# Sliding-window attention in four 64x64 tiles of the array, with the products with v beside the scores

## The chip, the cores and the metric

The kernel runs on one core of one Trainium2 chip. The metric is device time in microseconds of one execution, and less is better. A core has a matmul engine (TensorE, PE in the profile), a vector engine (VectorE, DVE), an engine for activations (ScalarE, ACT), a general one (GpSimd, POOL) and SyncE (SP), which here issues transfers. Matmuls write to PSUM, eight banks of 512 float32 columns in each of 128 partitions; everything else lives in SBUF.

## The reference

Attention with a sliding window of 128 and a linear distance penalty, then a gated feed-forward block. There are 8 batches of 8 heads, 576 positions and head dimension 64; the feed-forward width is 1536. Inputs and outputs are float32.

```python
scores = (q @ k.T) / sqrt(64) - slope[h] * abs(i - j)      # slope[h] = 2 ** -(h + 1)
scores = where((i - j >= 0) & (i - j < 128), scores, -1e9)
attn = softmax(scores)
x = (attn @ v) with heads side by side                     # 4608 tokens x 512
out = (gelu(x @ w_gate) * (x @ w_val)) @ w_out             # 4608 x 512
```

The window means that a key at position j meets only queries j to j + 127.

## The kernel before

Everything is in bfloat16 with float32 sums. The tokens go through the feed-forward block in nine groups of 512: a gate stage of 12 steps (`gate_val`, eight matmuls of 512 columns each) and an out stage (`out_part`, 16 units of three matmuls). The attention of the next batches is threaded between these. Scores are kept with keys on partitions and queries along the columns, so the exponentials serve as moving operand for the products with v without a transpose. Two heads lie over each other: `qT[64 * i : 64 * i + 64, c]` is head 2c + i.

Keys come in blocks of 128. A block meets 256 queries, and each head is one 64x128 tile, two of which run side by side:

```python
SCORES = (((0, 0, 256, 0), (1, 128, 256, 256)),          # key block, first query, queries, column
          ((2, 256, 256, 512), (3, 384, 192, 768), (4, 512, 64, 960)),
          ((2, 256, 256, 512), (3, 384, 128, 768), (3, 512, 64, 896), (4, 512, 64, 960)))

def scores(b, s, cs, then=None, later=None):
    for c in cs:
        ps = [bank(), bank()]
        for j, q0, n, col in SCORES[...]:
            for i in (0, 1):
                score(b, c, i, j, q0, n, ps[i][:, ...])
    ...                                     # per head pair: two exps of 512, one masking multiply
```

`exp` is an activation on ScalarE out of PSUM; `mask` multiplies by exp(-slope * distance), zero outside of the window, on VectorE. `add` adds on VectorE what two key blocks give to the same queries, so that the sums of the softmax need fewer matmuls:

```python
def sums(b, s):                             # column tiles of 128x32
    ...
    nc.vector.reciprocal(row(b)[:, lo:hi], ps[:, 0:hi - lo])

def gather(b, n=S):                         # reciprocals to DRAM
def spread_dma(b, n=S):                     # and back, broadcast over 64 partitions each

def products(b, s, cs):                     # 128x64 tiles, two side by side
    for c in cs:
        ps = bank()
        for n, (j, a, e, col) in enumerate(pieces):
            for i in (0, 1):
                h = 2 * c + i
                nc.tensor.matmul(out=ps[64 * i:64 * i + 64, a - lo:e - lo],
                                 lhsT=vb[b % 2][:, j, 64 * h:64 * h + 64],
                                 rhs=P[:, c, i, col:col + e - a], ...)
```

`values` multiplies the products by the reciprocals on VectorE and writes xT, the input of the gate stage. In batches 1 and 2 and in the first one the reciprocals are spread by small float32 matmuls (`spread4`, `sums4`) instead.

For batches from 2 on, q and k are loaded by GpSimd in five transfers each, converted on the way, and transposed by SyncE's transfer queue:

```python
def transposes_dma(b):
    for src, dst in ((ks, kT), (qs, qT)):
        nc.sync.dma_start_transpose(out=dst[b % 2]..., in_=src[b % 2]...)
```

The out stage of group g carries this (a number is that many out units; "s" are scores of batch, half and head pairs):

```python
todo = {
    0: [("s", 1, 0, (0, 1)), 4, ("s", 1, 0, (2, 3)), 2,
        ("s", 1, 1, (0, 1), None, masks), ("add", 1, 0), 2, ("sum4", 1, 0), ("masks",),
        ("s", 1, 1, (2, 3)), 4, ("spread4", 1, 0, acts), ("transposes", 2),
        ("sum4", 1, 1, False), ("pv", 1, 0), 2, ("spread4", 1, 1, acts), ("pv", 1, 1), 2],
    ...}
# groups 3 to 5, b = g + 2
    [("s", b, 0, (0, 1, 2)), 6, ("s", b, 0, (3,)), ("add", b, 0),
     ("s", b, 1, (0, 1)), ("add", b, 1, (0, 1)), 6, ("s", b, 1, (2, 3)), ("add", b, 1, (2, 3)), 4]
```

In those groups `sums` stands after gate step 1, `gather` after 3, `spread_dma` after 5, and the products with v after steps 8 and 10, two head pairs each.

Of the kernel before, what the change touches and what calls it, by code (L numbers as in the profile page):

```python
# [7 lines left out]
FP32 = mybir.dt.float32  # L8
# [10 lines left out]
SCORES = (((0, 0, 256, 0), (1, 128, 256, 256)),  # L19
          ((2, 256, 256, 512), (3, 384, 192, 768), (4, 512, 64, 960)),  # L20
          ((2, 256, 256, 512), (3, 384, 128, 768), (3, 512, 64, 896), (4, 512, 64, 960)))


PIECES = ((((0, 0, 256, 0), (1, 128, 384, 256), (2, 256, 384, 512)),
           ((2, 384, 512, 640), (3, 384, 576, 768), (4, 512, 576, 960))),
          (((0, 0, 256, 0), (1, 128, 256, 256)),
           ((2, 256, 512, 512), (1, 256, 384, 384), (3, 384, 576, 768), (4, 512, 576, 960))))
# [5 lines left out]
def kernel(  # L33
# [48 lines left out]

    slope1 = consts.tile([128, H], BF16, name="slope1")
    slopes = wo[:, 0:2, :].rearrange("p a (h x) -> p (a h) x", x=128)
    dist = wo[:, 2, 0:256]
    ones = consts.tile([128, 2, 32], BF16, name="ones")
    ones4 = consts.tile([128, 8 * 36], BF16, name="ones4")
    ones8 = consts.tile([128, 4 * 40], BF16, name="ones8")


    emask = consts.tile([128, H, 512], BF16, name="emask")
    sel0 = consts.tile([128, 8], FP32, name="sel0")
    sel = consts.tile([128, 8, 64], FP32, name="sel")
# [3 lines left out]
    qs, ks = ([consts.tile([128, 5, DM], BF16, name=f"{nm}s{i}") for i in range(2)]  # L97
# [8 lines left out]
    def load(t, src, b, js=range(5)):  # L106
        for j in js:
            n = rows(j)
            nc.gpsimd.dma_start(  # L109
                out=t[0:n, j, :].rearrange("p (h d) -> p h d", h=H),  # L110
                in_=src[b][:, 128 * j:128 * j + n, :].rearrange("h p d -> p h d"))

    def load_qk(b):
        load(qs[b % 2], q, b)
        load(ks[b % 2], k, b)

    def load_v(b, js=range(5)):
        load(vb[b % 2], v, b, js)
# [5 lines left out]
    def runs(what, b, n):  # L124
        first, parts, r = RUNS[b][n]
        t, lo, p = (qs, ks)[what][b], 1536 * n, 0
        if (b, n) == (0, 1):
            t, lo, p = vb[1], 0, 64 * what
        return t.rearrange("p j x -> p (j x)")[p:p + parts, lo:lo + 512 * r].rearrange(
            "p (h x) -> p h x", h=H)  # L130
# [40 lines left out]
    def transposes_dma(b):  # L171
        for src, dst in ((ks, kT), (qs, qT)):
            nc.sync.dma_start_transpose(
                out=dst[b % 2].rearrange("p c (j t) -> p (c j) t", t=128),
                in_=src[b % 2].rearrange("p j x -> p (j x)"))


    def columns(t, b, i, c, at, n):
        lo = 64 * i
        if b < 2:  # L180
            return t[b][lo:lo + 64, c, at:at + n]
        blocks = t[b % 2].rearrange("p c x -> p (c x)").rearrange(
            "p (j c t) -> p j c t", j=5, c=4)
        j = at // 128
        if n <= 128:
            return blocks[lo:lo + 64, j, c, at - 128 * j:at - 128 * j + n]
        return blocks[lo:lo + 64, j:j + n // 128, c, :]

    probs, both = {}, {}

    def prob(b):
        if b not in probs:
            probs[b] = p_pool.tile([128, 4, 2, 1024], BF16, name="P")
        return probs[b]

    def score(b, c, i, j, q0, n, out):
        rhs = columns(qT, b, i, c, q0, n)
        if rhs.ndim == 3:
            out = out.rearrange("p (n t) -> p n t", t=128)
        nc.tensor.matmul(out=out, lhsT=columns(kT, b, i, c, 128 * j, 128), rhs=rhs,  # L200
                         start=True, stop=True)
# [7 lines left out]
    def scores(b, s, cs, then=None, later=None):  # L209
        pss = []  # L210
        for c in cs:
            ps = [bank(), bank()]
            pss.append(ps)
            for j, q0, n, col in SCORES[s if b < 2 or s == 0 else 2]:
                for i in (0, 1):
                    score(b, c, i, j, q0, n, ps[i][:, col - 512 * s:col - 512 * s + n])
        if then:
            then()
        P = prob(b)
        for c, ps in zip(cs, pss):  # L220
            dst = P[:, c, :, 512 * s:512 * s + 512]
            for i in (0, 1):
                exp(dst[:, i, :], ps[i])
            if s == 0:
                args = (dst.rearrange("p i (n x) -> p i n x", n=2),
                        emask[:, 2 * c:2 * c + 2, 0:256].unsqueeze(2).to_broadcast(
                            (128, 2, 2, 256)))
            else:
                args = (dst, emask[:, 2 * c:2 * c + 2, :])
            if later is None:  # L230
                mask(*args)
            else:
                later.append(args)

    def bias(h, ps, n, start=True):
        d = dist.unsqueeze(1).to_broadcast((128, n, 256)) if n > 1 else dist[:, 0:128].unsqueeze(1)
        nc.tensor.matmul(out=ps.rearrange("p (n x) -> p n x", n=n),
                         lhsT=slopes[:, h, :], rhs=d, start=start, stop=False,  # L240
                         skip_group_check=True)

    def added(c, i, j, q0, n, out):
        nc.tensor.matmul(
            out=out, lhsT=columns(kT, 0, i, c, 128 * j, 128), rhs=columns(qT, 0, i, c, q0, n),
            start=False, stop=True, skip_group_check=True)


    def biases0(cs, idle=0):
        pss = []  # L250
        for c in cs:
# [3 lines left out]
            for i in (0, 1):  # L255
                bias(2 * c + i, ps[i], 2)
        return pss

    def scores0(cs, pss):
        for c, ps in zip(cs, pss):  # L260
            for j, q0, col in ((0, 0, 0), (1, 128, 256)):
                for i in (0, 1):
                    added(c, i, j, q0, 256, ps[i][:, col:col + 256])
# [5 lines left out]
    def scores0_rest(cs, later):  # L269
        pss = []  # L270
        for c in cs:
            ps = [bank(), bank()]
            pss.append(ps)
            for j, q0, n, col in ((2, 384, 128, 0), (3, 384, 192, 128), (4, 512, 64, 320)):
                for i in (0, 1):
                    score(0, c, i, j, q0, n, ps[i][:, col:col + n])
        P = prob(0)
        for c, ps in zip(cs, pss):
            for i in (0, 1):
                exp(P[:, c, i, 640:1024], ps[i][:, 0:384])  # L280
            later.append((P[:, c, :, 640:1024], emask[:, 2 * c:2 * c + 2, 128:512]))


    def biases0_2():
        pss = [bank(), bank()]
        for c in range(4):
            for i in (0, 1):
                bias(2 * c + i, pss[i][:, 128 * c:128 * c + 128], 1, c == 0)
        return pss

    def scores0_2(pss):
        for c in range(4):
            for i in (0, 1):
                added(c, i, 2, 256, 128, pss[i][:, 128 * c:128 * c + 128])
        for i in (0, 1):
            exp(prob(0)[:, :, i, 512:640], pss[i].rearrange("p (c n) -> p c n", c=4))
# [3 lines left out]
    def add(b, s, cs=range(4)):  # L300
        if b not in both:
            both[b] = s_pool.tile([128, 8, 448], BF16, name="S")
        lo, hi = 2 * cs[0], 2 * cs[-1] + 2
        P = prob(b).rearrange("p c i n -> p (c i) n")[:, lo:hi, :]
        T = both[b][:, lo:hi, :]

        def plus(out, in0, in1):
            nc.vector.tensor_tensor(out=out, in0=in0, in1=in1, op=ALU.add)  # L308

        if s == 0:  # L310
            plus(T[:, :, 0:128], P[:, :, 128:256], P[:, :, 256:384])
        else:
            by2 = P[:, :, 384:896].rearrange("p h (n y x) -> p h n y x", n=2, y=2)
            plus(T[:, :, 128:384].rearrange("p h (n x) -> p h n x", n=2),
                 by2[:, :, :, 0, :], by2[:, :, :, 1, :])
            plus(T[:, :, 384:448], P[:, :, 896:960], P[:, :, 960:1024])

# [13 lines left out]
    def shape(b, s):  # L331
        lo, hi = part(b, s)
        n = 4 if (b, s) == (0, 0) else 2
        return lo, (hi - lo) // n, n

    def sums4(b, s, added=True):
        first, w, count = shape(b, s)
        ps = bank()
        P, T = prob(b).rearrange("p c i n -> p (c i) n"), both.get(b)
        mms = []  # L340
        for h in range(H):
            for x in range(count):
                t = first + w * x
                g, lhsT = ((x, ones4[:, 32 * h:32 * h + 32]) if count == 4 else
                           (2 * x + h // 4, ones8[:, 32 * (h % 4):32 * (h % 4) + 32]))
                if added and t >= 128:
                    mms.append((g, lhsT, T[:, h, t - 128:t - 128 + w], 0, w, 0))
                elif added:
                    mms.append((g, lhsT, P[:, h, t:t + w], 0, w, 0))
                else:  # L350
                    for j, a, e, col in PIECES[min(b, 1)][s]:
                        lo, hi = max(a, t), min(e, t + w)
                        if lo < hi:
# [461 lines left out]
```

The softmax here doesn't subtract the row's maximum and nothing guards it: scores larger than these inputs give would overflow.

## Time and profile before

The median of three runs is 352.25 us (352.13 to 352.71). The profiled execution spans 350.6 us.

| stretch, us | what | length | PE busy | DVE busy | ACT busy |
|---|---|---|---|---|---|
| 0 to 18.66 | start, attention of batch 0 | 18.66 | 15.59 | 14.89 | 14.11 |
| 18.66 to 44.50 | gate stage of group 0 | 25.84 | 25.48 | 15.14 | 12.29 |
| 44.50 to 63.27 | out stage of group 0 | 18.77 | 18.65 | 13.60 | 13.84 |
| 63.27 to 104.97 | group 1 | 41.70 | 41.19 | 23.47 | 27.03 |
| 104.97 to 141.77 | group 2 | 36.80 | 36.80 | 25.80 | 22.42 |
| 178.19 to 214.61 | group 4 | 36.42 | 36.42 | 22.71 | 19.93 |
| 251.04 to 285.06 | group 6 | 34.02 | 34.02 | 15.61 | 10.80 |
| 285.06 to 316.14 | group 7, no attention | 31.08 | 31.08 | 8.30 | 9.51 |

The busy columns come from windows of the trace: time in which at least one instruction of that engine ran. A busy PE isn't a full PE, since the ends of its matmuls are modelled; what a stretch of it cost is read from the chain that ended last, where each piece runs until the next one starts. A group without attention lasts 31.08 us, so what a group lasts beyond that is its attention.

### The profile page before, as it was taken

The numbers are of one execution on the slowest core, as the hardware profiler recorded it, in microseconds if no ns is written. First come the engines' busy times: TensorE is split into PE (matmuls) and PEld (weight loads), VectorE is DVE, ScalarE is ACT, GpSimd is POOL, SyncE is SP. The second block draws the span as 40 slices with busy tenths as digits, with TensorE's granted clock in tenths as the row PEclk, the third lists the DMA queues.
The fourth block names the chain that finished last, engine by engine and source line by source line (L and its number), as shares of the span: only waits on it lengthen the run. The fifth ranks groups of instructions, "written<-read, shape, count | busy, mean of one in ns | idle before, by whom it ended". The sixth has DMA issues, their size and how long they took to land.

```text
span 350.6 us, 6847 instructions
## 1 busy us (share of the span) xinstructions
PE 343.2 (98%) x2756; PEld 171.4 (49%) x2756; DVE 193.6 (55%) x345; ACT 180.3 (51%) x332; POOL 105.7 (30%) x139
## 2 busy tenths in 40 slices
PE   8899999999999999999999999999999999999996
PEld 6665446444464445445444544454444544444443
DVE  6894467434878837856666655755684314303320
ACT  5963495535978374633863296328823123323322
POOL 9965480770850265003900292004000000000000
PEclk9999999999999999999999999999999999999999
DMA  9999999999999099984998399849206020021002
GB/s 180 173 197 190 202 154 165 187 152 160 144 152 182 3 168 182 197 164 54 155 226 148 68 145 196 179 93 97 92 6 133 30 90 3 1 82 39 0 30 90
DMA packets 148831, 43.00 MB, mean 123 GB/s; under 512 B 133784, under 2 KB 141720, under 8 KB 148800
## 3 DMA queue, kind: packets, MB, share of 16 engines
q0 software_dynamic: 108480, 18.49, 70.0%
q1 hardware_dynamic: 36976, 17.70, 21.3%
q10 hardware_dynamic: 3344, 6.38, 8.3%
q8 instruction: 21, 0.34, 0.4%
q14 instruction: 10, 0.08, 0.1%
HBM read 43.65 MB, written 9.53 MB: 152 GB/s over the span
## 4 chain that ended last, share of the span: by engine, by line
PE 91%; ACT 4%; DVE 3%; DMA 1%; issue 0%; ACTq 0%
PE ps L472 54%; PE ps L498 24%; PE ps L430 5%; PE ps L200 3%; ACT P L204 2%; PE ps L377 1%; PE ps L363 1%; DMA wo<-in_q_dram 1%; DVE P L207 1%; PE ps L399 1%; PE ps L514 1%; DVE S L308 1%; PE ps L152 0%; ACT qT L160 0%; ACT L204 0%; DVE xT L458 0%
## 5 line engine op out<-in xcount | busy, mean ns | idle before, releaser
L479 DVE TENSOR_TENSOR hT<-ps,gelu 128x512 bf16<-128x512 f32 (+3 forms) x112 | 73.8, 668 | 101.8 <-PE ps L472 94.8
L478 ACT ACTIVATE gelu<-ps 128x512 bf16<-128x512 f32 (+3 forms) x112 | 64.5, 582 | 114.8 <-PE ps L472 113.3
L472 PE MATMUL ps<-xT,wg 128*128 128x512 bf16 (+3 forms) x448 | 112.2, 372 | 0.5 <-DVE xT L444 0.2
L472 PE MATMUL ps<-xT,wv 128*128 128x512 bf16 (+3 forms) x448 | 111.6, 371 | 0.0
L498 PE MATMUL ps<-wo,hT 128*128 128x512 bf16 x420 | 95.6, 380 | 0.0
L204 ACT ACTIVATE P<-ps 128x512 bf16<-128x512 f32 (+1 forms) x130 | 65.9, 612 | 5.9 <-PE ps L200 4.9
L472 PEld LDWEIGHTS <-wv 128*128 128x128 bf16 x448 | 43.3, 98 | 50.3 <-issue 0.2
L472 PEld LDWEIGHTS <-wg 128*128 128x128 bf16 x448 | 42.0, 98 | 49.2 <-issue 1.8
L498 PEld LDWEIGHTS <-hT 128*128 128x128 bf16 x420 | 39.0, 98 | 46.5 <-issue 1.7
L207 DVE TENSOR_TENSOR P<-P,emask 128x1024 bf16<-128x1024 bf16 (+1 forms) x60 | 39.5, 679 | 24.1 <-ACT P L204 23.8
L503 ACT COPY osb<-ps 128x512 f32<-128x512 f32 x32 | 19.2, 599 | 35.4 <-PE ps L498 33.1
L109 POOL DMA_DIRECT2D vb<-in_v_dram x40 | 33.9, 883 | 3.9 <-DMA ks<-in_k_dram 1.9
L444 DVE TENSOR_TENSOR xT<-ps,rb 128x320 bf16<-128x320 f32 (+2 forms) x64 | 23.0, 423 | 11.4 <-DMA rb<-rd 6.8
L765 POOL COPY mark<-hT 1x2 bf16<-1x2 bf16 x4 | 0.7, 174 | 89.8 <-DVE hT L479 89.8
L109 POOL DMA_DIRECT2D qs<-in_q_dram x30 | 25.2, 857 | 7.4 <-DMA wo<-in_moe_w_out_dram 5.5
L109 POOL DMA_DIRECT2D ks<-in_k_dram x30 | 25.4, 891 | 6.1 <-DMA qs<-in_q_dram 6.0
L200 PE MATMUL ps<-qT,kT 64*128 64x256 bf16 (+3 forms) x352 | 18.6, 236 | 1.2 <-DVE xT L458 0.5
L404 DVE RECIPROCAL r<-ps 128x256 f32<-128x256 f32 (+1 forms) x10 | 18.8, 1921 | 0.0
L430 PE MATMUL ps<-P,vb 128*64 128x256 bf16 (+3 forms) x384 | 17.5, 239 | 0.0
L200 PEld LDWEIGHTS <-kT 64*128 64x128 bf16 x352 | 12.1, 94 | 11.1 <-issue 8.8
L430 PEld LDWEIGHTS <-vb 128*64 128x64 bf16 x384 | 14.7, 110 | 5.1 <-issue 4.6
L308 DVE TENSOR_TENSOR S<-P 128x1024 bf16<-128x1024 bf16 (+3 forms) x27 | 15.1, 590 | 0.5
(82 smaller groups left out, 138.3 us busy)
## 6 DMA issues: line engine op xcount, KB each, us to landing
out_dram<-osb SPq DMA_DIRECT2D x35, 256.0 KB, 3.5
rb<-rd ACTq DMA_DIRECT2D x10, 576.0 KB, 7.4
vb<-in_v_dram POOLq DMA_DIRECT2D x32, 128.0 KB, 6.3
qs<-in_q_dram POOLq DMA_DIRECT2D x24, 128.0 KB, 6.2
ks<-in_k_dram POOLq DMA_DIRECT2D x24, 128.0 KB, 6.3
wo<-in_moe_w_out_dram POOLq DMA_DIRECT2D x2, 768.0 KB, 14.7
wg<-in_moe_w_gate_dram POOLq DMA_DIRECT2D x5, 256.0 KB, 8.4
wv<-in_moe_w_val_dram POOLq DMA_DIRECT2D x5, 256.0 KB, 9.0
```

The source lines that it names most:

```text
L109: nc.gpsimd.dma_start(out=t[0:n, j, :].rearrange("p (h d) -> p h d", h=H), in_=src[b][:, 128 * j:128 * j + n, :].rearrange("h p d -> p h d"))
L200: nc.tensor.matmul(out=out, lhsT=columns(kT, b, i, c, 128 * j, 128), rhs=rhs, start=True, stop=True)
L204: nc.scalar.activation(out=dst, in_=src, func=AF.Exp, scale=0.125)
L207: nc.vector.tensor_tensor(out=dst, in0=dst, in1=m, op=ALU.mult)
L404: nc.vector.reciprocal(row(b)[:, lo:hi], ps[:, 0:hi - lo])
L430: nc.tensor.matmul(out=ps[64 * i:64 * i + 64, a - lo:e - lo], lhsT=vb[b % 2][:, j, 64 * h:64 * h + 64], rhs=P[:, c, i, col:col + e - a], s ...
L444: nc.vector.tensor_tensor(out=xT[:, c, at:at + e - a], in0=ps[:, a - lo:e - lo], in1=recip[b][:, c, a:e], op=ALU.mult)
L472: nc.tensor.matmul(out=ps, lhsT=w[:, c, 128 * f:128 * (f + 1)], rhs=xT[:, c, t0 + lo:t0 + hi], start=(c == 0), stop=(c == 3))
L478: nc.scalar.activation(out=gl[:, 0:n], in_=pg, func=AF.Gelu)
L479: nc.vector.tensor_tensor(out=hid[g][:, f, lo:hi], in0=pv, in1=gl[:, 0:n], op=ALU.mult)
L498: nc.tensor.matmul(out=acc[g], lhsT=hid[g][:, f, 128 * t:128 * (t + 1)], rhs=wo[:, f, :], start=(f == 0), stop=(f == NF - 1))
L503: (nc.vector.tensor_copy if t == 0 and g < 2 or t == 1 and g == 0 else nc.scalar.copy)(out=osb, in_=acc[g])
```

## The change

Keys are taken in nine blocks of 64 instead of five of 128. A block of 64 meets 192 queries, so less of what is computed falls outside of the window: 1664 columns of 64 keys for a head instead of 1024 of 128. A score matmul contracts over 64 and gives 64 keys, and so fills a quarter of the array: two heads by two key blocks run in four 64x64 tiles. The products with v likewise contract over 64 keys at a time, in four tiles: two halves of the keys' partitions by two heads. The two halves add into the same bank, and the kernel keeps them apart in time: each bank has first one half, then the other, and a relay on SyncE (a wait for the last matmul of the first half, then a signal) stands between them. The relay is a SyncE instruction, in program order with its transfers.

In the out stages of groups 2 to 5 the products with v now stand ahead of the first scores, in one stretch of 64x64 tiles, instead of in the gate stage. The diff is cut to its core; cuts are marked.

```diff
-SCORES = (...)
-PIECES = (...)
+COLUMNS = tuple(64 + 192 * n for n in range(5))
+COLUMNS0 = ((0, 192, 384), (None, None, 448, 640, 832))
...
-    qs, ks = ([consts.tile([128, 5, DM], BF16, ...) ...
+    qs, ks = ([consts.tile([128, 4, 5, 128], BF16, ...) ...
...
+    def load_qk(b):                        # two transfers for each block of rows, one per head of a pair
+        for t, src in ((qs[b % 2], q), (ks[b % 2], k)):
+            for j in range(5):
+                n = rows(j)
+                for i in (0, 1):
+                    nc.gpsimd.dma_start(
+                        out=t[0:n, :, j, 64 * i:64 * i + 64],
+                        in_=src[b][i:H:2, 128 * j:128 * j + n, :].rearrange("c p d -> p c d"))
...
+    def scores(b, s, cs, later=None):
+        for c in cs:
+            ps = [bank(), bank()]
+            for n in ((0, 1), (2, 3, 4))[s]:
+                w, col = 64 if n == 4 else 192, 192 * (n - 2 * s)
+                for x in (0, 1):
+                    for i in (0, 1):
+                        score(b, c, i, 2 * n + x, 128 * n + 64 * x, w,
+                              ps[i][64 * x:64 * x + 64, col:col + w])
+        w = (384, 448)[s]                  # width of an exp, 512 before
...
     def add(b, s, cs=range(4), alone=False):
+        for x in (0, 1):                   # each on 64 partitions
+            nc.vector.tensor_tensor(out=to[half, ...], in0=P[half, ...], in1=P[half, ...], op=ALU.add)
+            nc.vector.tensor_copy(out=to[half, ...], in_=P[half, ...])
...
+    def relay(mm):
+        by = nc.sync.nop()
+        depends(by, mm)
+        return by
...
+    def products(b, banks):
+        for n, (_, x, u, c, m, q0, q1, col, to) in enumerate(todo):   # in order of column, both halves
+            for i in (0, 1):
+                mm = nc.tensor.matmul(
+                    out=pss[u][64 * i:64 * i + 64, to:to + q1 - q0],
+                    lhsT=vb[b % 2][64 * x:64 * x + 64, m // 2, 64 * h:64 * h + 64],
+                    rhs=prob(b)[64 * x:64 * x + 64, c, i, col:col + q1 - q0], ...)
+                if begun[u] != x and u in by:
+                    depends(mm, by.pop(u))
+            if begun[u] == x and all(t[1:3] != (x, u) for t in todo[n + 1:]):
+                by[u] = relay(mm)
...
-                (nc.vector.tensor_copy if t == 0 and g < 2 or t == 1 and g == 0
+                (nc.vector.tensor_copy if g < B - 2 and t in by_dve.get(g, (0, 2))
                  else nc.scalar.copy)(out=osb, in_=acc[g])
...
-    ps0 = biases0_2()                      # a score pass of its own for queries 256 to 384 of batch 0
-    scores0_2(ps0)
...
-        0: [("s", 1, 0, (0, 1)), 4, ("s", 1, 0, (2, 3)), 2,
-            ...
-            ("s", 1, 1, (2, 3)), 4, ("spread4", 1, 0, acts), ("transposes", 2),
-            ("sum4", 1, 1, False), ("pv", 1, 0), 2, ("spread4", 1, 1, acts), ("pv", 1, 1), 2],
+        0: [("s", 1, 0, (0, 1)), 4, ("s", 1, 0, (2, 3)), 2, ("s", 1, 1, (0, 1)), ("add", 1, 1, (0, 1), True), 2,
+            ("sum4", 1, 0, lambda: scores(1, 1, (2, 3), masks), False), ("masks",),
+            ("add", 1, 1, (2, 3), True), 4,
+            ("spread4", 1, 0, acts), ("transposes", 2), 2, ("sum4", 1, 1), ("pv", 1, 0),
+            ("spread4", 1, 1, acts), ("pv", 1, 1), 2],
...
-        return [("s", b, 0, (0, 1, 2)), 6, ("s", b, 0, (3,)), ("add", b, 0),
-                ("s", b, 1, (0, 1)), ("add", b, 1, (0, 1)), 6, ("s", b, 1, (2, 3)),
-                ("add", b, 1, (2, 3)), 4]
+        if b == B:
+            return [4, ("pv", b - 1), 12]
+        return [("table",), 4, ("pv", b - 1), ("s", b, 0, (0,)), 4, ("s", b, 0, (1, 2, 3)), 4,
+                ("s", b, 1, range(4)), ("add", b, 0), ("add", b, 1), 4]
...
-                if f == (4 if g == 2 else 1):
-                    sums(g + 1, 0)
-                    sums(g + 1, 1)
+                if f == (4 if g == 2 else 2):
+                    sums4(g + 1, 0)
+                    sums4(g + 1, 1)
...
-                if g > 2 and f in (8, 10):
-                    for s in (0, 1):
-                        values(g + 1, s, (f - 8, f - 7))
```

`("table",)` is one small exp ahead of the out stage, which loads ScalarE's table for exp early. `sums` is gone; `sums4` is used for every batch, and in batch 0 and the first half of batches 1 and 2 it also works half by half with a relay between.

## The prediction

> **What bounds the kernel now.** I read the page first (busy shares), then the chain that ended last in order of time, then timelines of single stretches. TensorE (PE) is busy 98% of the span, at full granted clock throughout, so a microsecond counts only if it leaves PE's own stream or opens a hole in it.
>
> ```profile
> span 350.6 us, 6847 instructions
> PE 343.2 (98%) x2756; PEld 171.4 (49%) x2756; DVE 193.6 (55%) x345; ACT 180.3 (51%) x332; POOL 105.7 (30%) x139
> ```
>
> One steady group (here the fifth, 36.43 us) stands in the chain without a gap. Columns: start, length, engine and line, instructions. L472 is gate and value, L498 the out product, L399 the sums, L430 the products with v, L200 the scores.
>
> ```profile
> 214.61 3.45 PE ps L472 x16
> 218.07 0.61 PE ps L399 x24
> 218.68 12.19 PE ps L472 x56
> 230.87 1.01 PE ps L430 x24
> 231.88 3.56 PE ps L472 x16
> 235.44 1.01 PE ps L430 x24
> 236.44 1.83 PE ps L472 x8
> 238.28 0.76 PE ps L200 x12
> 239.04 3.99 PE ps L498 x18
> 243.03 0.77 PE ps L200 x20
> 243.80 3.99 PE ps L498 x18
> 247.79 0.55 PE ps L200 x16
> 248.34 2.69 PE ps L498 x12
> ```
>
> Sixteen 512-column matmuls in 3.45 us are 0.2156 us each, 0.421 ns a column. The 144 dense matmuls of a group are so 31.06 us. The rest, about 5.35 us, is attention: scores 0.76 + 0.77 + 0.55 = 2.08, v products 2.02, sums 0.61, and about 0.10 each time the dense stream is taken up again (12.19 for 56 that need 12.07; 3.56 for 16), six times. The attention work itself is, per batch, 8 heads x 1024 columns over two tiles = 1.73 us for scores, the same for v, and 0.49 for sums: 3.95 of 4.71. The other 0.76 over six insertions is 0.13 to enter. **An insertion costs about 0.23 us beside its columns.**
>
> The second place to look is SyncE's queue in the first out stage (start, length, engine, line, operation; in brackets the idle time before it and what ended it):
>
> ```profile
> 57.59 3.89 SPq L173 DMA_TRANSPOSE kT<-ks  x1
> 61.65 3.03 SPq L173 DMA_TRANSPOSE qT<-qs  x1
> 63.31 0.59 ACT L503 COPY osb<-ps 128x512 f32<-128x512 f32 x1 [1.24 <-PE ps L498]
> 64.78 0.61 SPq L507 DMA_DIRECT2D out_dram<-osb  x1
> ```
>
> The output tile was ready at 63.90, and its store left at 64.78, just after the second transpose released the queue at 64.68. A transpose holds SyncE for 3 to 4 us and whatever stands behind it waits; nothing on PE's path does so today.
>
> GpSimd's loads set when those transposes start:
>
> ```profile
> 44.51 0.87 POOL L109 DMA_DIRECT2D qs<-in_q_dram  x1 [2.90 <-DMA wo<-in_moe_w_out_dram]
> 45.87 1.56 POOL L109 DMA_DIRECT2D qs<-in_q_dram  x2 [0.48 <-issue]
> 47.48 4.25 POOL L109 DMA_DIRECT2D ks<-in_k_dram  x5
> L109 POOL DMA_DIRECT2D qs<-in_q_dram x30: 692/883/913, 37.2 to 203.4; - x30
> ```
>
> The last k load is issued by 51.73 and lands about 6 us later, when the transpose at 57.59 starts. The last line gives min/median/max of an issue: a 64-row one takes 0.69, a 128-row one 0.88.
>
> **What the Trainium skill says.** "TensorEngine Tiling (Array Packing)", Tiling Modes: tiles work independently, and a change of tiling mode drains the array. The trace agrees: two tiles run near their column count, and each change costs the 0.1 to 0.23 above. "PSUM — Partial Sum Buffer", PSUM bank collisions: different row tiles must not write one bank at the same time, software has to order them. No run here shows it; it is why the change adds relays. "TensorE: Matmul & The Clock Gate", Part 1: after an idle window of about 3.4 us the clock falls to half until PE has been busy that long again. PE's gaps here are all 1.0 us or less, so this trace doesn't show it.
>
> **The change part by part, steady groups.** Scores: 8 x 1664 columns over four tiles = 3328 x 0.421 = 1.40 us, and v: the order that keeps the two row halves in different banks ends at column 3456 = 1.46 us (1920 columns first, then 1536). Four 128-column sum matmuls already follow each other at about 13 ns in the timeline, so issue should keep up with four tiles of 192 columns (20 ns). Sums stay 0.49. Insertions fall from six to four, because v and the first scores share one. Without new waits: 1.40 + 1.46 + 0.49 + 4 x 0.235 = 4.29 us against 5.35: **minus 1.05 a group.** But I see three waits:
> - The second half of v waits for a relay on SyncE. In program order the relays stand behind the store of the first output tile, which waits for its VectorE copy: 0.11 (start after the last out matmul, as such copies show) + 0.69 + 0.03 + 0.33 for the issue = 1.2 us with the relay. PE is there at 0.13 + 0.81 = 0.94. Wait 0.28.
> - The last scores take 8 banks, all there are. The eighth is the third output tile's, whose copy stands on VectorE behind four masks. These wait for eight exps of about 0.4 us (512-wide ones follow each other at 0.51). Wait about 0.35.
> - The sums after the third gate step need the adds of both halves, now eight VectorE operations, about 4.6 us (64-partition adds at 0.66 to 1.0, copies about 0.4). Wait about 0.15.
>
> With all three a group is 5.07, minus 0.28. I take half way and a bit less: minus 0.5 each for groups 3 to 5, minus 0.7 for group 2 (its 36.8 was longer), minus 0.3 for group 6 (one insertion less). ScalarE's exps get narrower and two of four output copies go to VectorE; both have idle time, so no gain from that.
>
> **Start and groups 0 and 1.** The start loses the extra bias and score pass for queries 256 to 384 (16 matmuls and two exps, about 1.1 us at 10.7 to 12.3) and gains relays: minus 0.5. Groups 0 and 1 each gain about 0.35 on scores, about as much again on v if no relay is late, and some insertions: minus 0.9 and minus 1.0. All gains together: 0.5 + 0.9 + 1.0 + 0.7 + 1.5 + 0.3 = **4.9 us**.
>
> **The cost that I expect to decide.** In group 0 the program places both transposes of batch 2 on SyncE ahead of the relays of the first v product of batch 1. PE can't pass that point until both transposes are issued, and these need all 20 new q and k loads (ten before, twice as many issues for the same bytes). Loads: the third issue stays at 44.5 (it waits for a lane that the w_out load holds). Then 17 more at 0.69 end at 56.3, at 57.7 if lanes limit; landing 3.4 (the least seen) to 6.3: about 60.5. Then 3.89 + 0.17 + 3.03: SyncE is free at 67.6. PE, from 45.2: scores and out steps 0.44 + 2.8 + 0.44 + 1.4 + 0.5 + 1.4, sums with scores between about 1.3, out 2.7, spread 0.7, out 1.4, sums 0.7 (with a wait for the adds), half of v 0.35: about 59.2, and 58.8 with the gain at the start. **Hole of 8.8 us.** It is longer than 3.4 us, so by the clock page PE comes back at half speed for some 3 us: 1.3 us more, an estimate from that page. Sum: 352.25 - 4.9 + 8.8 + 1.3 = 357.4; I say 357.0.
>
> **Rivals.**
> (a) The hole is absent or short and tiles bring their full gain: 4 x 1.05 and about 3.5 elsewhere, 344 to 347. For it: three of the four kinds of matmul already run near their column count. Against it: the SyncE order and the measured 3.0 to 3.9 us of a transpose; even with loads landing as early as now (57.6), SyncE is free at 64.7 and PE waits about 5.9.
> (b) Only the loads are as quick as before: hole 5.9, clock 1.2, gains 4.9: 354.5.
> (c) Four tiles don't run side by side, being bound by weight loads (64-column ones take 110 ns in the page against 98 for 128): then scores and v stay at about 2 us each, gains shrink to 2, and 360 to 362 follows.
> (d) VectorE becomes the bound: it was busy 22.5 of 36.4 us in a steady group, and adds about 2 us of adds and 1.4 of copies, saves 1.7 on reciprocals (two of 128 and 160 columns for two of 256 and 320). It remains far from full; it can only cause the local waits above.
>
> **Range and chances.** The hole, 5.9 to 10.5 with its clock loss, and gains, 2 to 8.5, are the two large terms, largely independent: 350 to 363.5 should hold 8 times in 10. 2% is 7.0 us. Faster by over 2% needs rival (a) whole: 0.05. Slower needs over 359.3: 0.28. Within: 0.67.
>
> **What would show it.** The chain after: steady groups of 35.4 to 36.2 us with four insertions, v and first scores joined in one of about 2.1 us. In the waits, PE's weight load of the v product waiting several us once, at about 59 us, for SyncE; the transposes of batch 2 at about 60.5 in SyncE's timeline; granted clock below 1.00 just behind. Shown wrong by: no PE hole near 59 us; steady groups unchanged at 36.4 (tiles not parallel) or under 35.4 (waits that I put in absent); a hole elsewhere, for instance where the v product waits for late reciprocals.

## The result, and the profile after

The changed kernel takes **365.19 us** (median of four runs, 363.74 to 365.72) against 352.48 us for the kernel before on the same chip. The ratio is 1.035 (95% interval 1.030 to 1.039): **slower by 3.5%**, above the predicted 357.0 us and above its range.

The head of the page after:

```profile
span 363.8 us, 8340 instructions
...
PE 344.4 (95%) x3436; PEld 174.2 (48%) x3436; DVE 196.0 (54%) x359; ACT 166.9 (46%) x328; POOL 143.3 (39%) x202
...
PEclk9999999589999999999999999999999999999999
```

PE's busy time is almost what it was (343.2 before), but the span is 13.2 us longer: the time went into idleness, and the granted clock, full throughout before, falls in the eighth and ninth slices. The timeline of PE shows that place (start, length, engine and line, operation, count; in brackets the idle time before, and what ended it). L411 is the products with v, L353 the spread of the reciprocals, L499 the out product, L470 gate and value:

```profile
59.49 0.46 PE L411 MATMUL ps<-P,vb 64*64 64x192 bf16 x16
69.49 0.74 PE L411 MATMUL ps<-P,vb 64*64 64x192 bf16 x16 [9.53 <-SPq L314]
70.16 1.84 PE L353 MATMUL ps<-r,sel 32*128 32x160 f32 x16
71.93 1.92 PE L411 MATMUL ps<-P,vb 64*64 64x64 bf16 x56
73.78 1.93 PE L499 MATMUL ps<-wo,hT 128*128 128x512 bf16 x6
75.55 0.81 PE L470 MATMUL ps<-xT,wg 128*128 128x512 bf16 x3
```

PE stops for 9.53 us between the two halves of the first products with v, until SyncE's relay (L314). The six out matmuls behind it take 1.77 us, from 73.78 to 75.55; at full clock six take 1.40. One line of the chain and two of SyncE's timeline say what the relay stood behind:

```profile
58.25 4.56 DMA ks<-in_k_dram
63.01 3.12 SPq L167 DMA_TRANSPOSE kT<-ks  x1
66.19 3.12 SPq L167 DMA_TRANSPOSE qT<-qs  x1
```

The last load of k lands at 62.8. Only then can SyncE issue the two transposes of batch 2, and they hold its queue until 69.3. The relay is behind them.

In the steady groups the new waits are small. This is the chain in group 4 (start, length, what), with the out stage's first and third output tile:

```profile
215.38 0.70 DVE osb L504
216.08 0.02 issue
216.10 0.33 SPq L508
...
216.54 0.95 PE ps L411 x31
...
223.85 0.70 DVE osb L504
224.54 0.04 issue
224.59 0.38 PE ps L181 x8
```

VectorE copies an output tile, SyncE issues its store, and only then comes the relay for the second half of the products with v. Further on the last eight score matmuls wait for the copy of another output tile, whose bank they take.

Where the 13.2 us lie, read as the starts of the gate stages in both traces:

| stretch | before, us | after, us | difference |
|---|---|---|---|
| start and group 0 (to the gate of group 1) | 63.11 | 75.55 | +12.44 |
| group 1 | 41.86 | 42.88 | +1.02 |
| group 2 | 36.63 | 36.35 | -0.28 |
| groups 3, 4, 5 | 36.43, 36.42, 36.42 | 36.37, 36.35, 36.36 | -0.19 |
| group 6 | 34.02 | 33.99 | -0.03 |

The other 0.24 us lie behind group 6.

### The profile page after: what moved, and what is told of

It is laid out like the page before. It is cut to its first block, busy times and chain, and to the rows that moved or that the text cites. A ratio compares the mean times of both kernels' runs of the same rounds, so it can differ in the third digit from the quotient of the medians.

```text
span 363.8 us, 8340 instructions
## 1 busy us (share of the span) xinstructions
PE 344.4 (95%) x3436; PEld 174.2 (48%) x3436; DVE 196.0 (54%) x359; ACT 166.9 (46%) x328; POOL 143.3 (39%) x202
## 3 DMA queue, kind: packets, MB, share of 16 engines
HBM read 43.65 MB, written 9.53 MB: 146 GB/s over the span
## 4 chain that ended last, share of the span: by engine, by line
PE 77%; DMA 7%; ACT 5%; POOL 3%; DVE 3%; SPq 2%; issue 2%; ACTq 0%; POOLq 0%; DVEq 0%
PE ps L470 47%; PE ps L499 20%; DMA wo<-in_moe_w_out_dram 4%; ACT P L186 4%; PE ps L411 3%; PE ps L181 2%; SPq L167 2%; POOL ks L104 2%; PE ps L339 2%; POOL qs L104 2%; DVE osb L504 2%; PE ps L353 1%; DMA ks<-in_k_dram 1%; ACT osb L504 1%; DMA wo<-in_q_dram 1%
## 5 line engine op out<-in xcount | busy, mean ns | idle before, releaser
L470 PE MATMUL ps<-xT,wg 128*128 128x512 bf16 (+3 forms) x448 | 112.2, 372 | 0.5 <-DVE xT L442 0.3
L470 PE MATMUL ps<-xT,wv 128*128 128x512 bf16 (+3 forms) x448 | 111.6, 372 | 0.0
L499 PE MATMUL ps<-wo,hT 128*128 128x512 bf16 x420 | 96.6, 381 | 0.0
L470 PEld LDWEIGHTS <-wv 128*128 128x128 bf16 x448 | 43.4, 98 | 50.2 <-issue 0.2
L470 PEld LDWEIGHTS <-wg 128*128 128x128 bf16 x448 | 42.8, 98 | 49.7 <-issue 0.7
L186 ACT ACTIVATE P<-ps 128x384 bf16<-128x384 f32 (+2 forms) x128 | 56.1, 542 | 21.2 <-PE ps L181 20.9
L499 PEld LDWEIGHTS <-hT 128*128 128x128 bf16 x420 | 39.2, 98 | 47.1 <-issue 0.7
L104 POOL DMA_DIRECT2D qs<-in_q_dram x60 | 43.1, 758 | 7.8 <-DMA wo<-in_moe_w_out_dram 4.7
L189 DVE TENSOR_TENSOR P<-P,emask 128x768 bf16<-128x768 bf16 (+1 forms) x60 | 34.4, 588 | 18.0 <-ACT P L186 17.8
L104 POOL DMA_DIRECT2D ks<-in_k_dram x60 | 43.5, 833 | 0.0
L442 DVE TENSOR_TENSOR xT<-ps,rb 128x512 bf16<-128x512 f32 (+3 forms) x49 | 21.7, 509 | 22.0 <-PE ps L411 19.7
L411 PE MATMUL ps<-P,vb 64*64 64x192 bf16 (+2 forms) x704 | 18.3, 235 | 10.8 <-SPq L314 10.4
L411 PEld LDWEIGHTS <-vb 64*64 64x64 bf16 x704 | 14.5, 112 | 16.0 <-SPq L314 11.6
L181 PE MATMUL ps<-qT,kT 64*64 64x192 bf16 (+2 forms) x656 | 19.4, 236 | 1.2 <-issue 0.6
L271 DVE TENSOR_TENSOR T<-P 64x1024 bf16<-64x1024 bf16 (+3 forms) x28 | 18.9, 675 | 0.6
L344 DVE RECIPROCAL r<-ps 128x128 f32<-128x128 f32 (+3 forms) x16 | 16.1, 1035 | 2.2 <-PE ps L339 2.1
```

The source lines that it names most:

```text
L104: nc.gpsimd.dma_start(out=t[0:n, :, j, 64 * i:64 * i + 64], in_=src[b][i:H:2, 128 * j:128 * j + n, :].rearrange("c p d -> p c d"))
L181: nc.tensor.matmul(out=out, lhsT=kT[b % 2][half, c, 64 * m:64 * m + 64], rhs=qT[b % 2][half, c, q0:q0 + n], start=first, stop=True, skip_g ...
L186: nc.scalar.activation(out=dst, in_=src, func=AF.Exp, scale=0.125)
L189: nc.vector.tensor_tensor(out=dst, in0=dst, in1=m, op=ALU.mult)
L411: mm = nc.tensor.matmul(out=pss[u][64 * i:64 * i + 64, to:to + q1 - q0], lhsT=vb[b % 2][64 * x:64 * x + 64, m // 2, 64 * h:64 * h + 64], r ...
L442: nc.vector.tensor_tensor(out=xT[:, c, at:at + e - a], in0=src, in1=recip[b][:, c, a:e], op=ALU.mult)
```

## The experiments

All times are medians beside runs of the kernel before on the same chip, which took 352.5 to 352.9 us in every set. Theory: one relay in SyncE's order behind two slow transposes makes the hole, and smaller waits of the same kind use up what the four tiles save. Rivals: the four tiles don't run side by side; the number of loads, not the order, makes the hole; the clock, not the hole, costs most. Most ratios are known to some 0.2 to 0.4%, so medians that lie within 1 us of each other aren't told apart; there the lengths of the groups in the traces, each from one execution, have to do.

### The transposes behind the products with v

```diff
-            ("spread4", 1, 0, acts), ("transposes", 2), 2, ("sum4", 1, 1), ("pv", 1, 0),
-            ("spread4", 1, 1, acts), ("pv", 1, 1), 2],
+            ("spread4", 1, 0, acts), 2, ("sum4", 1, 1), ("pv", 1, 0),
+            ("spread4", 1, 1, acts), ("pv", 1, 1), ("transposes", 2), 2],
```

> The changed kernel with one item moved: in the out stage of group 0 both transposes of batch 2 stand behind the v products of batch 1. If the hole at 59.5 us comes from the relays standing behind the transposes on SyncE, it goes, and with it the half clock behind it: 365.2 - 9.5 - 2.4 = 353.3 us, granted clock 1.00, steady groups unchanged at 36.36. If instead the v product waited for something else that only ends then (late v loads, late exps), a hole of several us stays near 59 us and the time stays over 360.

Measured: 358.98 us (357.04 to 360.28), ratio 1.017 [1.013, 1.021]. The hole is gone and the gate of group 1 starts at 64.33, 11.2 us earlier. So the order on SyncE made it. But the kernel gained only 6.2 us, because group 1 now takes 47.04 us and not 42.88. PE's timeline shows why, and then SyncE's:

```profile
95.86 0.52 PE L339 MATMUL ps<-P,ones 64*32 64x64 bf16 x24 [2.76 <-SPq L314]
86.00 4.84 SPq L167 DMA_TRANSPOSE kT<-ks  x1
90.90 3.76 SPq L167 DMA_TRANSPOSE qT<-qs  x1
```

The relay of the sums of batch 2 now stands behind the transposes of batch 3. In the changed kernel this second meeting is hidden: the hole pushed PE 12 us back, past these transposes. The granted clock was 0.50 from about 96.5 to 100 us, behind a gap of 2.76 us.

### The relays on ScalarE's queue

```diff
-        by = nc.sync.nop()
+        by = nc.scalar.nop()
```

> The changed kernel with the relays on ScalarE instead of SyncE, transposes and stores where they were. ScalarE has nothing to do where most v products need their relay. If SyncE's order is the whole story, both costs go: the hole with its clock loss (11.9 us) and the 0.4 us wait in each of groups 2 to 5 (behind the store of the first output tile): 365.2 - 11.9 - 1.6 = 351.7 us, steady groups 36.0. If a relay's own length (matmul end to semaphore to semaphore) sets the wait in the steady groups, they stay at 36.3 and the time is about 353.

Measured: 356.69 us (353.32 to 357.56), ratio 1.008 [1.004, 1.011]. No hole at 59 us either, and without moving a transpose: this confirms the queue. Steady groups take 35.99 us where nothing else waits (two of four). The others, 36.56 and 36.32, lost 0.43 us at gelu, behind transfers of the reciprocals that ScalarE issues, and 0.14 and 0.33 at the sums. Group 1 again lost time, 45.1 us: there the scores of batch 3 waited 1.09 us for `qT<-qs`, the transpose itself, and the clock was 0.50 from about 106 to 109 us. So batch 3 is late, whoever carries the relays.

### The hole filled with idle matmuls

42 matmuls of zeros into a spare bank stand where the hole is, so that PE is busy through it.

```diff
+            if b == 1 and begun[u] != x and not filled:
+                filled.append(bank())
+                for _ in range(42):
+                    nc.tensor.matmul(out=filled[0], lhsT=zeros, rhs=wg[:, 0, 0:512], ...)
```

> The changed kernel with 42 matmuls of zeros (512 columns, result unused) put before the first v product that waits for a relay, about 9.1 us of work inside of the 9.5 us hole. The hole in useful work stays. If the half clock behind the hole costs what the slow stretch suggests (69.5 to 75.6 us took about 2.4 us more than its instructions need), the time falls to about 362.9 with a clock of 1.00 in every slice; if the slow stretch has another cause, it stays at 365.

Measured: 363.62 us (two runs, 363.24 and 364.01), ratio 1.031 [1.027, 1.034]. From the second half of the products to the gate of group 1 there are 4.21 us here (69.04 to 73.25), at a granted clock of 1.00, against 6.06 in the changed kernel (69.49 to 75.55):

```profile
59.87 9.24 PE L414 MATMUL ps<-wg,zeros 128*128 128x512 bf16 x42
69.04 0.46 PE L418 MATMUL ps<-P,vb 64*64 64x192 bf16 x16
...
73.25 1.03 PE L477 MATMUL ps<-xT,wg 128*128 128x512 bf16 x4
```

**The lower clock behind the hole costs 1.85 us**; it is a consequence of the hole, not the main loss. The whole kernel is only 1.6 us faster, and measures the clock less well: the fill itself held PE until 69.04, when SyncE had been free since 68.06.

### Half of the loads

The heads with odd numbers of q and k of batch 2 aren't loaded (zeros in their place), so that the output for batch 2 is not the reference's. The first form set the zeros on VectorE:

```diff
-                for i in (0, 1):
+                for i in (0,) if b == 2 else (0, 1):
...
+        nc.vector.memset(t[:, :, :, 64:128], 0.0)
```

> The changed kernel without the second of the two transfers of each row block of q and k of batch 2 (its odd heads are zeros instead, so half of that batch's scores are left out of what is computed): 10 loads instead of 20. If the doubled number of loads delays the transposes, the last k load is issued near 51.5 instead of 58.2 us, the transposes start near 56.5 instead of 63.0, the hole falls from 9.5 to about 3 us, and the time to about 357. If the transfers' bytes or landing set it, the transposes start less than 3 us earlier and the time stays over 361.

Measured: 366.71 us (364.37 and 369.05). As a time it says little: VectorE's memset waited for GpSimd and held the gate stage of group 0, so PE came to the products 4 us late. The hole was 5.04 us. The second form sets the zeros on GpSimd (`nc.gpsimd.memset` in the last line):

> The changed kernel with the odd heads of q and k of batch 2 not loaded (zeros from two GpSimd memsets in their place), 10 loads instead of 20, so that the output for batch 2 is not the reference's. It measures how much of the hole at 59 us comes from the number of loads. Theory: GpSimd needs 0.72 to 0.79 us per load whatever its size, so that the last load lands some 5 us earlier (at 57 to 58 us instead of 62.8), both transposes end near 64 instead of 69.3 and the hole is 4 to 5 us instead of 9.5; kernel 358 to 360. Rival: the transfers are limited by the bytes or by the loads of wo and v before them; then half the loads land under 2 us earlier and the hole stays above 7.5.

Measured: 362.92 us (362.27 and 363.58), ratio 1.027 [1.021, 1.034]. In PE's timeline the hole, and in SyncE's the transpose and what stood ahead of it:

```profile
66.72 0.74 PE L411 MATMUL ps<-P,vb 64*64 64x192 bf16 x16 [5.10 <-SPq L314]
52.11 7.64 SPq L508 DMA_DIRECT2D out_dram<-osb  x3
60.01 3.34 SPq L167 DMA_TRANSPOSE kT<-ks  x1
```

With ten loads the hole is 5.10 us instead of 9.53, just above the expected 4 to 5. The loads make it longer, by 4.4 us; the order makes it. But here the loads no longer set when the transposes start. The last one was issued by 51.94, and SyncE then stood at the third store: it was issued from 59.42 to 59.75, as soon as its tile was copied (58.81 to 59.40), and the first transpose followed at 60.01. PE's own progress sets that store, so when PE is later, as in the first form, the hole moves with it and stays near 5 us. The kernel's time missed the expected 358 to 360: it came down by only some 2 us, since PE was 1.7 us later at this place in the profiled run (1.3 us of it from the gate stage of group 0, where the clock was 0.50 from about 18.5 to 22 us) and the clock still fell to 0.50 at the hole. The run halved the bytes along with the number of loads, so it doesn't tell these two apart. GpSimd's time for a load does depend on size: 0.74 us for 128 rows of half the heads and 0.62 for 64 rows here, 0.88 for 128 rows of all heads in the kernel before.

### The loads of batch 3 without their wait

On top of the first experiment, the GpSimd copy that held them back until the keys of batch 2 were transposed is left out:

```diff
-            nc.gpsimd.tensor_copy(out=mark, in_=kT[0][0:1, 0, 0:2])
             load_qk(3)
```

> The transposes of batch 2 stand behind the products with v of batch 1 (as in the run with the transposes moved behind), and the loads of batch 3 no longer wait for the transposed keys of batch 2 (the GpSimd copy to mark is left out): they follow the loads of batch 2 directly. Theory: the 4.2 us that the run with the transposes moved still lost in group 1 (47.0 us against 42.9) came from a second meeting of the same kind, the transposes of batch 3 at 86 to 95 us ahead of the relay of the second half of the sums of batch 2, and the lower clock after it. Then group 1 takes 42 to 43 us again and the kernel 354 to 355.5. Rival 1: the time in group 1 is lost to something that does not hang on when the transposes run; then group 1 stays at 47 and the kernel at 359. Rival 2: the earlier loads of batch 3 take bandwidth from those of batch 2 or from the rest; then group 0 ends later and the kernel stays above 356.

Measured: 354.88 us (354.54 to 358.43), ratio 1.006 [1.004, 1.009]. Group 1 takes 42.88 us again, and the transposes of batch 3 run from 80.6 instead of 86.0. The second meeting is confirmed. What remains is 2.3 us above the kernel before: start and group 0 end 1.2 us later (64.31 against 63.11), group 1 costs 1.0 more.

### The store behind the relays

On top of that, the store of the first output tile is issued after the relays, in groups 2 to 6.

```diff
+        while stores:                      # at the end of products()
+            r0, osb = stores.pop()
+            nc.sync.dma_start(out=out[r0:r0 + 128, :], in_=osb)
```

> As the run with the third batch early, and in groups 2 to 5 the store of the first output tile is issued on SyncE behind the relays of the products with v, not ahead of them. Theory: of the 2.46 us of the products with v and the first scores in a steady group, 0.4 is a relay that stands behind a store, which itself waits for VectorE's copy (0.70). Then this stretch takes 2.04 to 2.1, four groups gain 0.35 to 0.4 each, and the kernel takes 1.4 to 1.7 us less than with the third batch early alone. Rival: the 0.4 is the way of the two signals through any queue; then the stretch stays at 2.4 and the two times agree.

Measured: 353.76 us (352.69 to 356.77), ratio 1.002 [1.001, 1.004]. PE's timeline, the products with v and what follows them and the first scores:

```profile
171.57 1.83 PE L411 MATMUL ps<-P,vb 64*64 64x192 bf16 x83
...
173.56 2.76 PE L503 MATMUL ps<-wo,hT 128*128 128x512 bf16 x11
```

From 171.57 to 173.56 are 1.99 us; the same stretch of the changed kernel took 2.38 (215.27 to 217.65). A steady group falls from 36.36 to 35.98 us, as expected, and group 6 from 33.99 to 33.72. The medians differ by 1.1 us, where 1.4 to 1.7 was expected.

### Scores between the halves

On top of the third batch early (without the moved store): the first scores stand between the two halves of the products, and ScalarE copies the third output tile.

```diff
+            if between and by and at >= mid:
+                between()                  # scores of the first pair of heads
+                between = None
...
-                (nc.vector.tensor_copy if g < B - 2 and t in by_dve.get(g, (0, 2))
+                (nc.vector.tensor_copy if g < B - 2 and t in by_dve.get(g, (0,))
```

> As the run with the third batch early, and in the steady groups the scores of the first pair of heads stand between the two halves of the products with v, so that the relay has some 0.5 us of other matmuls beside it, and the third output tile is copied by ScalarE, not by VectorE. Theory: both waits of a steady group are covered: products with v and first scores 2.05 instead of 2.46 us, last scores 0.9 instead of 1.24; a steady group takes 35.6 instead of 36.36 and the kernel 3 to 3.5 us less than with the third batch early alone, some 351 to 352. Rival: the banks come free later with products and scores side by side (eight banks, seven in use), and ScalarE, with eight exponentials in front of the copy, frees the bank no earlier; then the waits only move, a group stays at 36.2 to 36.4 and the kernel gains under 0.8.

Measured: 355.25 us (354.38 to 357.09), ratio 1.008 [1.004, 1.011]; no gain in the medians. In the traces a steady group takes 36.11 us instead of 36.36, where 35.6 was expected. Products and first scores take 2.21 us (168.36 to 170.57) instead of 2.38, but still more than 1.99 with the store moved; the scores now interrupt the products. The last scores went only from 1.24 to 1.19. So the theory held for a part of the first wait and failed for the second; here a relay was better made early than covered.

### The third output tile copied in two halves

On top of the store behind the relays:

```diff
+                if 2 <= g < B - 2 and t == 2:
+                    nc.scalar.copy(out=osb[:, 0:256], in_=acc[g][:, 0:256])
+                    nc.vector.tensor_copy(out=osb[:, 256:512], in_=acc[g][:, 256:512])
```

> As the run with the store behind the relays, and in groups 2 to 5 the third output tile is copied half by ScalarE and half by VectorE side by side (0.35 us or so each in place of one copy of 0.69), so that the last of the eight score banks is free some 0.3 us earlier. With ScalarE alone copying it (0.58), the last scores only went from 1.24 to 1.19. Theory: the length of the copy, not the engine, is the wait: last scores 0.9 to 1.0, a steady group 35.7 instead of 35.98, the kernel 0.8 to 1.2 us less than with the store behind the relays alone (353.8). Rival: the scores of eight banks are limited by something else (their exponentials free the earlier banks too late); then 1.24 stays and the times agree.

Measured: 353.24 us (352.77 to 355.66), ratio 1.002 [1.000, 1.004]; a steady group 36.03, the last scores 1.30. The halves did not run side by side: VectorE's began 0.40 us after ScalarE's, so the bank came free no earlier. Whether a shorter copy helps stays untested by this.

### The last scores apart

On top of the moves in group 1 (next), three out matmuls stand between the third and the fourth pair of the last scores:

```diff
-                ("s", b, 1, range(4)), ("add", b, 0), ("add", b, 1), 4]
+                ("s", b, 1, range(3)), 1, ("s", b, 1, (3,)), ("add", b, 0), ("add", b, 1), 3]
```

> As the run with the moves in group 1, and in groups 2 to 5 three matmuls of the fourth output tile stand between the first three pairs and the fourth pair of the last scores, so that the copy of the third output tile has some 0.65 us more before its bank is wanted again. Theory: the last scores wait some 0.3 us for this bank (1.24 us where 48 matmuls of the kind that takes 0.62 for 24 would need some 1.0), and the wait goes; the extra change between two kinds of matmul costs 0.1 to 0.2, so that a steady group takes 35.7 to 35.9 instead of 35.97 and the kernel 0.3 to 1 us less than with the moves in group 1 alone (352.8). Rival: eight banks of scores take 1.24 us because of the matmuls themselves (pace of the columns and the change of kind); then the two pieces take together 1.35 to 1.45 and the kernel is 0.5 to 1 us slower.

Measured: 352.82 us (351.01 to 354.86), ratio 1.001 [0.999, 1.002]. Four lines of PE's timeline; and the wait that came in a later group:

```profile
174.95 0.78 PE L181 MATMUL ps<-qT,kT 64*64 64x192 bf16 x36
175.67 0.82 PE L503 MATMUL ps<-wo,hT 128*128 128x512 bf16 x3
176.42 0.39 PE L181 MATMUL ps<-qT,kT 64*64 64x192 bf16 x12
176.74 2.12 PE L503 MATMUL ps<-wo,hT 128*128 128x512 bf16 x9
197.19 1.02 PE L473 MATMUL ps<-xT,wg 128*128 128x512 bf16 x4 [0.35 <-ACT gelu L479]
```

The two pieces take 0.72 and 0.32, 1.04 us together, with one more change of kind in it, where one piece took 1.25. So the bank was the wait. But the four groups last 144.5 us in sum, as they did with the moves in group 1 alone (144.3). The scores of a group took 0.2 us less and its out matmuls 0.1 more. In one group 0.5 us was lost at gelu, behind a transfer of the reciprocals that ScalarE issues, and in two others the sums took 0.77 and 0.98 us instead of 0.62; with the moves in group 1 alone, one group had such a delay (0.88).

### The moves in group 1

On top of the store behind the relays, the sums' relay goes by ScalarE in groups 0 and 1, and in group 1 out matmuls cover the wait for the reciprocals.

```diff
-                by = relay(mm)
+                by = relay(mm, nc.scalar if b else nc.sync)
...
-            ("spread4", 2, 0, acts), ("s", 3, 0, (0, 1), masks), 2, ("sum4", 2, 1), ("pv", 2, 0),
-            ("spread4", 2, 1, acts), ("s", 3, 0, (2, 3), masks), ("pv", 2, 1), 2, ("masks",),
+            ("spread4", 2, 0, acts), ("s", 3, 0, (0, 1), masks), 2, ("sum4", 2, 1), ("pv", 2, 0), 1,
+            ("spread4", 2, 1, acts), ("s", 3, 0, (2, 3), masks), ("pv", 2, 1), 1, ("masks",),
```

> As the run with the store behind the relays, and in groups 0 and 1 the relay of the sums goes by ScalarE's queue, not SyncE's, and in group 1 three of the last six out matmuls stand between the first products with v and the spread of their sums, to cover the wait for the reciprocals. Theory: the sums' relay stops costing 0.28 to 0.31 us in each of the two groups, and the 0.45 us wait for the reciprocals in group 1 goes; group 1 takes 42.1 to 42.4 instead of 42.88, the kernel about 1 us less than with the store behind the relays alone. Rival: the adds and reciprocals on VectorE set the pace of these groups; then the wait comes back at the next products or at the gate, and under 0.4 us is gained.

Measured: 352.79 us (351.57 to 354.39), ratio 1.000 [0.998, 1.002]. Group 1 takes 42.02 us instead of 42.88, where 42.1 to 42.4 was expected. With the copy in two halves as well:

> Both moves of the two runs above in one kernel. If both theories hold and add up: 353.8 - 1.0 - 1.0 = 351.8, just below the kernel before the change (352.6). If only one holds: 352.8. If neither: 353.8.

Measured: 352.48 us (351.77 to 354.54), ratio 0.999 [0.997, 1.001]. This is the lowest median of all, and it can't be told from the kernel before. **The whole loss can be taken back by order, queues and one wait left out; a gain beyond that wasn't found.**

## Why the prediction was wrong

**The bound.** TensorE's own stream sets the time, and a hole in it counts whole: right. The 9.53 us hole is in the span.

**The hole: right in place and cause, and near in size.** Predicted 8.8 us at 59 us, with SyncE free at 67.6; measured 9.53 us at 59.9, with SyncE free at 69.3. The order on SyncE was the cause, as the first two experiments show. The size was in part luck: SyncE was free 1.7 us later than predicted, and PE arrived 1.1 us later too. The loads landed at 62.8 and not at 60.5: GpSimd's loads of q started at 44.80, 45.75, 46.71, 47.69 and 49.08, with 1.32 us of gaps, of which the profile puts 0.24 to an earlier transfer; those of k took 0.72 us each where the prediction had 0.69; and its sum left out the third load's own 0.69 (44.5 + 18 × 0.69 is 56.9, not 56.3). The two transposes took 6.3 us, 0.8 less than predicted. The reading that the loads set the transposes in the kernel before doesn't hold as it stands: there, too, the transpose at 57.59 came right behind a store, issued from 56.99 to 57.32. Rival (b), loads as quick as before, is answered by the run with half of them: 5.10 us of hole, set by that store, against the 5.9 of its sum.

**The clock: right in kind, too small.** Predicted 1.3 us, shown 1.85. PE worked at 0.50 for 5.3 us (69.49 to about 74.8), where the prediction had some 3.

**The gains: this step failed.** The prediction gave 4.9 us; the trace has a loss. Start to group 1's gate is 12.44 us longer, of which the hole and the clock explain 9.53 + 1.85 = 11.38. The remaining 1.06 is a loss where 0.5 + 0.9 of gain stood: the start gained 0.16, the gate stage of group 0, which carries the rest of batch 0, lost 0.57, and the out stage 0.65. Group 1 lost 1.02 where a gain of 1.0 stood. Groups 2 to 6 gained 0.28 + 0.19 + 0.03 = 0.50, where 2.5 stood. In sum a loss of 1.6 instead of a gain of 4.9: **6.5 of the 7.8 us** between the 357.4 of its sum and the result. The rest is the hole (0.7) and the clock (0.55).

**Why groups 0 and 1 lost.** The out stage of group 1, each piece of PE's timelines counted from its start to the start of the next:

| kind | before, us | after, us |
|---|---|---|
| scores | 5.15 | 4.65 |
| sums | 1.15 | 1.29 |
| products with v | 2.35 | 3.39 |
| spread | 1.42 | 1.76 |
| out matmuls | 10.98 | 10.98 |

Scores gained 0.50, more than the 0.35 of the prediction. The same line took products with v to gain as much "if no relay is late", and they lost 1.04. 0.45 us of that is a wait for the reciprocals, because sums, products and spread now stand directly behind each other; the out matmuls that once lay between stand elsewhere. The scores' row of after also contains a wait of 0.28 us for the relay of the sums. The run with both places changed took back 0.86 us. So the step took the saved columns and didn't look at what the new order uncovers. Of the rest of the products' loss, some 0.6 us, 0.15 is a wait for exponentials; the remainder wasn't taken apart. Group 0 has the same two waits: with the transposes moved, its out stage took 18.93 us against 17.89, with 0.31 for the relay of the sums and 0.47 for the reciprocals in it. The lines of the two waits in group 1:

```profile
104.60 0.52 PE L339 MATMUL ps<-P,ones 64*32 64x64 bf16 x24 [0.28 <-SPq L314]
112.11 1.17 PE L353 MATMUL ps<-r,sel 32*128 32x160 f32 x16 [0.45 <-DVE r L344]
```

**The steady groups.** The waits of the prediction were read well in sum, and leaving them half out was the main error. The wait behind the store was put at 0.28, and the run with the store moved took 0.38 off each group. The last scores were predicted at 0.9 + 0.35 and took 1.24; the run with them apart shows the bank to be the wait. The third one, sums behind the adds, put at 0.15, didn't come here: they took 0.62 us, as before (in other runs single groups show 0.14 to 0.36). With its three waits the prediction had 0.28 of gain for a group, then "half way and a bit less" to the full 1.05 made 0.5 of it. Measured were 0.06. What is left between 0.28 and 0.06 is the joined stretch: even with its wait gone, products and first scores took 1.99 us, where the prediction's own terms give 1.75 (1.46 for the products, 8 × 192 / 4 × 0.421 ns = 0.16 for the scores, 0.13 to enter). Why wasn't taken apart.

**Rivals.** (c), four tiles that don't run side by side, is refuted: 24 score matmuls of 192 columns take 0.62 us with the entry into the stretch (220.34 to 220.96), 26 ns each; one alone at the prediction's 0.421 ns a column would take 81:

```profile
220.34 0.69 PE L181 MATMUL ps<-qT,kT 64*64 64x192 bf16 x24
...
220.96 2.76 PE L499 MATMUL ps<-wo,hT 128*128 128x512 bf16 x12
```

(a) falls with the hole, and (d), VectorE as the bound, was right to be limited to local waits.

## What to carry to other kernels

A signal that an engine carries for others stands in program order with everything else of that engine: before placing one, list what its queue holds ahead of it and when each of these can go. After a large hole is mended, look at the trace again, since the delay can have hidden a second one. And where an order changes, count the waits that the old order covered before counting what the shorter instructions save.

## What the runs showed beyond the expected

The prediction cited the Trainium skill ("TensorE: Matmul & The Clock Gate", Part 1) for an idle window of about 3.4 us. In five profiled runs the granted clock fell to 0.50 without a gap that long:

- with the transposes moved, from about 96.5 to 100 us, after a gap of 2.76 us that had ended at 95.86;
- with the store behind the relays, from about 13 to 19.8 us, at the end of a gap of 1.93 us (to 13.63);
- in both runs with half of the loads, for some 3 us from 18 to 18.5 us on, around gaps of 1.19 and 1.26 us (to 18.00 and 18.27);
- with the relays on ScalarE, from about 106 to 109 us, when the last gaps, of 1.09 and 0.42 us, had ended at 99.45 and 103.1.

Gaps of 1.19 us (the last scores apart) and 1.33 us (scores between the halves) at the same place left it at 1.00, so the length of a gap doesn't decide alone. The kernel before, with no gap over 1.00 us in its profile, isn't free of this either: of its 40 runs beside the third batch early, five had a mean granted clock of 0.994 or 0.995 and took 353.85 to 356.00 us. What lowers the clock in these runs stays open.
